# Another issue order for an attention and two-MoE kernel: 100 planning passes, three disturbed replays, mended instruction costs

## The chip, the cores and the metric

The kernel runs on one core of a Trainium2 chip. A core has a matmul engine (TensorE, PE in the profile; its weight loads are listed as PEld), VectorE (DVE), ScalarE (ACT), GpSimd (POOL) and SyncE (SP), which here issues the DMA transfers. Each engine works through its own queue in a fixed order; engines wait for each other through semaphores. The metric is the device time of one execution in microseconds (us).

## The reference

```python
# q, k, v: (4, 8, 576, 64) float32
q_d = q.reshape(B, H, Sd, 4, D).mean(axis=3)      # k_d, v_d alike: sequence pooled by 4
out_d = softmax(q_d @ k_d.T / sqrt(D)) @ v_d
out_up = np.repeat(out_d, 4, axis=2)
mask = np.abs(pos[:, None] - pos[None, :]) < 4    # a band of +-3
out_local = softmax(where(mask, q @ k.T / sqrt(D), -1e9)) @ v
x = (out_up + out_local) as (2304 tokens, 512)
# MoE1: w_in (512, 2048), w_out (2048, 512), alpha (2048)
h = x @ w_in
x = (np.maximum(h, 0) + alpha * np.minimum(h, 0)) @ w_out
# MoE2: w_gate, w_val (512, 1536), w_out (1536, 512), rms_g (512)
xn = x / sqrt(mean(x * x) + 1e-6) * rms_g
g = xn @ w_gate
out = (g * sigmoid(g) * (xn @ w_val)) @ w_out
```

The weights arrive as 64-bit floats and are decoded on the chip.

## The kernel before

**Numbers.** The large products take fp32 operands as two fp16 parts, high and low, and do three fp16 matmuls (high x high, high x low, low x high). Making the two parts is called a split: ACT writes the high part (line 373), DVE the low one (line 374).

**Weights.** A piece of a weight matrix (768 KB of 64-bit floats for the larger ones) is loaded as pairs of 32-bit words by SP (line 1091, tile `wr`), its high words are scaled by ACT (line 1110), its low words by ACT (line 1113), DVE joins the two (line 1115, tile `wc`) and the piece is then split into the tiles `wi`, `wo`, `w` or `w2` that the matmuls read. Lines 1110 and 1113 together are called the decode pair of a piece.

**Stages.** In the first 100 us, attention of batch 0 runs mostly on TensorE: q and k are loaded (line 743, tile `wo`), transposed by TensorE into PSUM tiles `tps` (line 792), written to SBUF by ACT (line 793, tile `T`), scored (lines 815, 868 to 880), exponentiated by ACT (lines 825, 900, tiles `dd` and `dls`) and multiplied with v. The local attention of batches 1 to 3 is done by DVE and POOL (products L478 and L526, sums L489 and L539), spread between later work. MoE1 takes blocks of 192 or 384 tokens: `hps` = x @ w_in on TensorE (line 1371), `g` on ACT (1375), alpha on DVE (1377), a split, and a second product (1388). MoE2 takes blocks of 384 tokens: `gps` on TensorE (1488), `th` = tanh on ACT (1497), DVE (1499, 1502), a split (1508, 1509, tile `uhl`) and the product with w_out (1517); the output leaves at 1586.

**What sets the order.** The program is first written in a natural order. Then `issue_order` (from line 24, called at 1715) orders every engine's queue anew. It works out which instruction needs which, gives each a cost (`cost`), and plays the whole program through repeatedly: a pass back from the end gives priorities, a pass forward gives a schedule whose times feed the next pass. In the forward pass it also models the matmul engine's slow periods and the port that DVE and POOL share. The order of the pass that ends first is kept, and each engine's queue is chained in it (`add_manual_dep`), the DMA queue of SP too. So the numbers in `cost` and the choice of pass set the order, and nothing else of the program.

Of the kernel before, what the change touches and what calls it, by code (L numbers as in the profile page):

```python
# [20 lines left out]
    return bass.AP(tensor=ap.tensor, offset=ap.offset + off, ap=[p] + [list(d) for d in dims])  # L21


def issue_order(tc, nc, groups, rounds=40):


    insts = [i for i in nc.cur_bb.bb.instructions if i.opcode != "TilePoolBoundary"]
    count = range(len(insts))
# [6 lines left out]
    def free(a):  # L35
        n = 1
        for _, c in list(a.ap)[1:]:
            n *= c
        return n
# [7 lines left out]
    def wide(a):  # L47
        return 2 if "16" in str(a.dtype) else 4

    def psum(a):  # L50
        return "PSUM" in str(a.tensor.space)

    def span(a):
        if psum(a):
            return 0, 128, 0, 1 << 20
        p, lo = divmod(a.offset, row(a))
        hi = lo + 1 + sum(abs(s) * (n - 1) for s, n in list(a.ap)[1:])
        return p, p + a.ap[0][1], lo * wide(a), hi * wide(a)
# [19 lines left out]
    def transfer(o, i):  # L78
        sides = [[c for _, c in a.ap if c > 1] or [1] for a in (o, i)]
        rings = max(x for x in range(1, 17) if not any(s[0] % x for s in sides))  # L80
        n = max(runs(a)[0] for a in (o, i))
        each = 4.0 * min(runs(a)[1] for a in (o, i))
        share = n / 16 * (10.0 + 0.046 * each)
        return max(share, n / rings * (9.0 + 0.042 * each)), max(share, 600.0)

    def cost(k, ins, outs):
        i, e = insts[k], eng[k]
        if not outs:
            return 60.0
        o, n = outs[0], free(outs[0])  # L90
        if e == "SP":
            return transfer(o, ins[0])[0]
        if e == "PE":
            if wide(ins[0]) == 2:
                return n / 2.4 + (2.5 if n > 128 else 50)
            return n * 2 / 2.4 + 4 if i.is_transpose else n * 4 / 2.4 + 100
        n = max([n] + [free(a) for a in ins[:1]])
        extra = len([a for a in ins[1:] if free(a) == 1 and n > 1])
        if e == "Activation":
            return (51 if psum(ins[0]) else 93) + n / 1.2 + 93 * (extra + len(outs) - 1)  # L100
        if e == "DVE":
            if i.opcode == "Reciprocal":
                return 89 + 6.25 * n
            fast = i.opcode in ("TensorScalarPtr", "TensorCopy") and not any(psum(a) for a in ins)
            fast = fast and len([a for a in ins if free(a) > 1]) < 2
            return 89 + n / (1.92 if fast else 0.96) + 60 * (extra > 0)
        if i.opcode == "TensorTensor":
            return 148 + n * (1.667 if any(list(a.ap)[-1][0] == 0 for a in ins) else 2.104)
        return 36 + 0.83 * n if i.opcode == "Memset" else 370 + 6 * n if i.opcode == "ISA" else 200 + 2.0 * n

    aps = [tuple([a.bass_ap for a in l if hasattr(a, "bass_ap")] for l in (i.ins, i.outs)) for i in insts]
    dur = [cost(k, *aps[k]) for k in count]

    held = [transfer(aps[k][1][0], aps[k][0][0])[1] if eng[k] == "SP" and aps[k][1] else None for k in count]

    def second(k, ins):
        if eng[k] == "Pool":
            return bool(ins)
        if eng[k] != "DVE" or not ins:
            return False  # L120
        n = len([a for a in ins if free(a) > 1 and not psum(a)])
        if n > 1:
            return True
        return insts[k].opcode in ("TensorScalarPtr", "TensorCopy") and not any(psum(a) for a in aps[k][0] + aps[k][1])

    shared = [second(k, aps[k][0]) for k in count]
# [6 lines left out]
    for names in ring.values():  # L133
        names = sorted((n for n in names if n in users), key=lambda n: users[n][0])
        kept = []
        for x, n in enumerate(names):
            old = {users[names[x - 1]][0]} if x else set()
            if len(kept) == slots[n]:
                done = [h for h in kept if users[h][-1] < users[n][0]]
# [5 lines left out]
    preds = [set() for _ in count]  # L145
    writes, reads, bank, first = {}, {}, {}, {}
    for k, (ins, outs) in enumerate(aps):
        for l, wr in ((ins, False), (outs, True)):
            for a in l:
                n = a.tensor.name  # L150
                if n not in slots:
                    continue
                s = span(a)
# [18 lines left out]
    succs = [[] for _ in count]  # L172
    at = {i.name: k for k, i in enumerate(insts)}
    mate, joined, fixed = {}, set(), [0.0] * len(insts)
# [22 lines left out]
    def lag(a, b):  # L197
        return 2300 if eng[a] == "SP" else waits.get((eng[a], eng[b]), 100)

    engines = sorted(set(eng))  # L200
    WIN, BUSY = 3413.0, 2900
    work = [0 if eng[k] != "PE" or not aps[k][1] else
            free(aps[k][1][0]) * (1 if wide(aps[k][0][0]) == 2 or insts[k].is_transpose else 2) for k in count]

    def run(P, S, prio, fwd, d):
# [33 lines left out]
                        heapq.heappush(soon[eng[s]], (at[s], s))  # L239
        return end, seq, real  # L240

    prio, d, best = [float(-k) for k in count], dur, None
    for _ in range(rounds):
        end = run(succs, preds, prio, False, d)[0]
        end, seq, d = run(preds, succs, [-x for x in end], True, dur)
        prio = [-x for x in end]
        if best is None or max(end) < best[0]:
            best = max(end), seq
    info = mybir.DependencyInfo(mybir.DependencyClass.NoSync, mybir.DependencyReason.DATA)
    for q in best[1].values():  # L250
        for a, b in zip(q, q[1:]):
# [4 lines left out]
def kernel(  # L256
# [1453 lines left out]
    for kind, m in (("m2", 0), ("m2", 1), ("m1", 2), ("m1", 3), ("m2", 2), ("m2", 3), ("m1", 4), ("m1", 5), ("m2", 4), ("m2", 5)):  # L1710
        if kind == "m1":
            m1(m, 0, BW, sl((kind, m)))
        else:
            m2(m, sl((kind, m)))
    issue_order(tc, nc, groups)


# [28 lines left out]
```

## Time and profile before

| | |
|---|---|
| median of 3 runs | 969.99 us (968.99 to 970.92) |
| the profiled execution | 967.56 us, of which its span 965.8 us |
| mean granted matmul clock | 0.991 of full speed |
| PE busy | 929.6 us (96% of the span) |
| DVE busy | 685.5 us (71%) |
| ACT busy | 481.7 us (50%) |
| POOL busy | 117.5 us (12%) |
| moved by DMA | 73.80 MB, 76 GB/s on average |

Busy shares are averages over the whole span, and the stages differ: which engine is full in which stretch is to be read from the stretches themselves. The median of the runs is 2.4 us above the profiled execution.

### The profile page before, as it was taken

What the parts mean: (1) busy time and instruction counts of PE and PEld (TensorE: products, weight loads), DVE (VectorE), ACT (ScalarE), POOL (GpSimd) and SP (SyncE); (2) the same over time, 40 slices, a digit from 0 to 9 for tenths busy, and PEclk for the clock granted to TensorE, in tenths of its full rate; (3) what the DMA queues carried; (4) which work ended last, traced back from release to release, by engine and by line L of the source; (5) the groups of instructions that cost most, each with busy time, mean ns of one, the idle gap of its engine ahead of it and who ended that gap; (6) DMA issues with size and microseconds to landing.
All of it is one profiled execution on the core that took longest, in us unless ns stands there. A gap on an engine that the chain in (4) does not pass through costs nothing.

```text
span 965.8 us, 16581 instructions
## 1 busy us (share of the span) xinstructions
PE 929.6 (96%) x6484; PEld 600.2 (62%) x6484; DVE 685.5 (71%) x1447; ACT 481.7 (50%) x1108; POOL 117.5 (12%) x96
## 2 busy tenths in 40 slices
PE   6978999999999999999999999999999999999998
PEld 4767777799655555565566655555556666555554
DVE  4789996998999978999987899963333442542333
ACT  5999889889864273233575322221322433321322
POOL 1101100201021103333102313210000000000000
PEclk9978999999999999999999999999999999999999
DMA  8886534574302142122122211000000000000000
GB/s 207 253 274 181 161 100 137 197 226 155 128 1 58 52 141 95 44 72 62 45 85 73 82 38 36 22 22 1 20 14 1 1 1 1 1 1 10 24 1 33
DMA packets 53712, 73.80 MB, mean 76 GB/s; under 512 B 22190, under 2 KB 35138, under 8 KB 53634
## 3 DMA queue, kind: packets, MB, share of 16 engines
q1 hardware_dynamic: 53634, 72.74, 24.9%
q8 instruction: 51, 0.84, 0.4%
q14 instruction: 27, 0.22, 0.1%
HBM read 68.01 MB, written 4.72 MB: 75 GB/s over the span
## 4 chain that ended last, share of the span: by engine, by line
PE 67%; DVE 13%; ACT 9%; issue 6%; DMA 5%; POOL 0%; SPq 0%; ACTq 0%; POOLq 0%
PE gps L1488 23%; PE hps L1371 12%; PE acc L1388 12%; PE oacc L1517 11%; DMA out_dram<-ob 4%; DVE prod L539 2%; DVE ls L489 1%; ACT wr L1110 1%; ACT dls L900 1%; DVE prod L526 1%; ACT wr L1113 1%; ACT wi L373 1%; DVE ghl L374 1%; DVE prod L478 1%; DVE hps L1377 1%
## 5 line engine op out<-in xcount | busy, mean ns | idle before, releaser
L1371 PE MATMUL hps<-xt,wi 128*128 128x192 f16 (+1 forms) x1536 | 357.0, 290 | 7.2 <-DVE g L374 3.8
L1488 PE MATMUL gps<-x,w 128*128 128x384 f16 x1728 | 339.0, 326 | 3.3 <-DVE th L1499 3.0
L1388 PE MATMUL acc<-ghl,wo 128*128 128x384 f16 (+1 forms) x960 | 253.8, 310 | 1.7 <-DVE ghl L374 0.6
L1488 PEld LDWEIGHTS <-w 128*128 128x128 f16 x1728 | 169.9, 99 | 118.4 <-issue 5.2
L1517 PE MATMUL oacc<-w,uhl 128*128 128x512 f16 x630 | 191.5, 379 | 2.3 <-ACT ob L1573 1.6
L1371 PEld LDWEIGHTS <-wi 128*128 128x128 f16 x1536 | 149.5, 100 | 59.4 <-issue 7.3
L1388 PEld LDWEIGHTS <-wo 128*128 128x128 f16 x1344 | 129.0, 98 | 61.7 <-issue 4.5
L1377 DVE SCALAR_TENSOR_TENSOR hps<-g,oma,hps 128x192 f32<-128x192 f32 (+1 forms) x128 | 66.0, 516 | 61.3 <-ACT g L1375 61.0
L1497 ACT ACTIVATE th<-gps,tsc 128x384 f32<-128x384 f32 x72 | 41.8, 580 | 132.3 <-PE gps L1488 131.8
L1517 PEld LDWEIGHTS <-uhl 128*128 128x128 f16 x630 | 61.6, 98 | 67.3 <-issue 2.4
L1499 DVE SCALAR_TENSOR_TENSOR th<-th,gps 128x384 f32<-128x384 f32 x72 | 39.6, 550 | 87.8 <-ACT th L1497 87.4
L1375 ACT ACTIVATE g<-hps 128x384 f32<-128x384 f32 x96 | 47.3, 493 | 84.1 <-PE hps L1371 83.5
L1508 ACT ACTIVATE uhl<-gps 128x384 f16<-128x384 f32 x72 | 41.7, 579 | 94.3 <-DVE gps L1502 85.5
L478 POOL TENSOR_TENSOR prod<-cq,ckv 128x896 f32<-128x896 f32 x24 | 54.8, 2284 | 191.6 <-DVE ls L489 50.6
L1388 PE MATMUL acc<-g,wo 128*128 128x384 f16 (+1 forms) x384 | 70.4, 286 | 0.0
L373 ACT ACTIVATE ghl<-hps,grp 128x384 f16<-128x384 f32 (+1 forms) x73 | 42.0, 576 | 51.2 <-DVE hps L1377 48.6
L1509 DVE TENSOR_TENSOR uhl<-gps,uhl 128x384 f16<-128x384 f32 x72 | 45.3, 629 | 28.1 <-ACT uhl L1508 27.8
L526 POOL TENSOR_TENSOR prod<-ls,ckv 128x896 f32<-128x896 f32 x24 | 43.6, 1816 | 163.3 <-DVE lo L539 70.6
L539 DVE TENSOR_TENSOR prod<-prod 128x384 f32<-128x384 f32 (+1 forms) x96 | 59.4, 630 | 4.3 <-POOL prod L526 4.3
L374 DVE SCALAR_TENSOR_TENSOR ghl<-hps,grp,ghl 128x384 f16<-128x384 f32 (+1 forms) x73 | 44.3, 607 | 23.9 <-ACT ghl L373 23.6
L489 DVE TENSOR_REDUCE ls<-prod 128x14 f32<-128x896 f32 x48 | 51.1, 1075 | 0.1
L1110 ACT ACTIVATE wr<-wr 128x768 f32<-128x768 f32 (+1 forms) x48 | 41.8, 877 | 6.2 <-DMA wr<-in_moe_w_out_dram 3.2
(242 smaller groups left out, 1138.9 us busy)
## 6 DMA issues: line engine op xcount, KB each, us to landing
wr<-in_moe_w_out_dram SPq DMA_DIRECT2D x18, 512.0 KB
wr<-in_moe_w_in_dram SPq DMA_DIRECT2D x10, 768.0 KB
wr<-in_moe_w_gate_dram SPq DMA_DIRECT2D x8, 768.0 KB
wr<-in_moe_w_val_dram SPq DMA_DIRECT2D x8, 768.0 KB
ckv<-in_k_dram SPq DMA_DIRECT2D x7, 768.0 KB
ckv<-in_v_dram SPq DMA_DIRECT2D x7, 768.0 KB
wr<-in_moe_w_out_dram SPq DMA_DIRECT2D x20, 256.0 KB
sd<-in_q_dram SPq DMA_DIRECT2D x24, 144.0 KB
```

What stands on the lines that cost most here:

```text
L373: nc.scalar.activation(out=hi, in_=src, func=AF.Copy, scale=s)
L374: nc.vector.scalar_tensor_tensor(out=lo, in0=src, scalar=s, in1=hi, op0=ALU.mult, op1=ALU.subtract)
L478: engs[i].tensor_tensor(out=pr, in0=view(st["q"][:, j, t:t + TP], [[D, TP], [0, ND], [1, D]]), in1=view(st["k"][:, j, t:t + TP], [[D, TP], ...
L489: nc.vector.tensor_reduce(out=st["s"][:, j, t:t + TP], in_=st.pop(("p", i)), axis=AX.X, op=ALU.add)
L526: engs[i].tensor_tensor(out=pr, in0=view(st["s"][:, j, t:t + TP], [[ND, TP], [1, ND], [0, D]]), in1=view(st["v"][:, j, t:t + TP], [[D, TP] ...
L539: add = lambda o, a, c: nc.vector.tensor_tensor(out=o, in0=a, in1=c, op=ALU.add)
L1110: nc.scalar.activation(out=hi.bitcast(F32), in_=hi.bitcast(F32), func=AF.Prelu, scale=2.0 ** -112, alpha=2.0 ** 32)
L1371: nc.tensor.matmul(ps[:, j], wi[:, f + j, a, kk * 128:(kk + 1) * 128], x[:, b_, kk, c0:c0 + n], start=(i == 0), stop=(i == 3 * KK - 1))
L1377: nc.vector.scalar_tensor_tensor(out=ps[:, j], in0=g[:, j], scalar=oma[:, f + j:f + j + 1], in1=ps[:, j], op0=ALU.mult, op1=ALU.add)
L1388: nc.tensor.matmul(acc[e], wo_f(f)[:, a, e * 128:(e + 1) * 128], hl[:, b_], start=(f == f0 and i == 0), stop=(f == f1 and i == 2))
L1488: nc.tensor.matmul(ps, w2_t[i0 + f // 3].rearrange("p a (k c) -> p a k c", k=KK)[:, a, kk, (f % 3) * 128:(f % 3 + 1) * 128], xh[:, b_, kk] ...
L1517: nc.tensor.matmul(acc[tt], t[:, a, tt * 128:(tt + 1) * 128], w[:, b_, f % 3], start=(f in first and i == 0), stop=(f in last and i == 2))
```

## The change

Only `issue_order` is changed; lines behind it stand 35 further down in the new file (L793 becomes L828, L374 becomes L409). Three things are new: 100 passes in place of 40; costs of some kinds of instruction (small fp16 and fp32 matmuls, transposes, ACT reading with a stride or writing 16 bits, DVE reading PSUM with a stride, and a floor for short DVE instructions); and the choice among the passes, which takes those that end less than 8 us after the best mean so far, plays their orders through three times with disturbed costs of ACT, DVE and SP, and keeps the order with the least mean end. No instruction is added or removed on any engine.

```diff
-def issue_order(tc, nc, groups, rounds=40):
+def issue_order(tc, nc, groups, rounds=100):
...
-                return n / 2.4 + (2.5 if n > 128 else 50)
-            return n * 2 / 2.4 + 4 if i.is_transpose else n * 4 / 2.4 + 100
+                return max(25.0, n / 2.4 + 2.5)
+            return n * 2 / 2.4 + 3 if i.is_transpose else n * 4 / 2.4 + (128 if n < 64 else 8)
...
-            return (51 if psum(ins[0]) else 93) + n / 1.2 + 93 * (extra + len(outs) - 1)
+            odd = ins and not psum(ins[0]) and list(ins[0].ap)[-1][0] != 1
+            return ((51 if psum(ins[0]) else 93) + n / (1.09 if odd else 1.2) + 93 * (extra + len(outs) - 1)
+                    + 20 * (wide(o) == 2))
...
-            return 89 + n / (1.92 if fast else 0.96) + 60 * (extra > 0)
+            if ins and psum(ins[0]) and list(ins[0].ap)[-1][0] > 2:
+                return 69 + n / 0.58
+            return max(150, 69 + n / (1.92 if fast else 0.96) + 60 * (extra > 0))
...
+    def replay(seq, factors, phase):
+        by = dict(zip(("Activation", "DVE", "SP"), factors))
...
+            f = by.get(e, 1.0)
+            x = f * dur[k]
...
+    trials = (((1.0, 1.0, 1.0), 0.0), ((1.03, 1.0, 1.1), 1700.0), ((1.0, 1.03, 0.95), 800.0))
...
-        if best is None or max(end) < best[0]:
-            best = max(end), seq
+        if best is None or max(end) < best[0] + 8000.0:
+            x = sum(replay(seq, *a) for a in trials) / len(trials)
+            if best is None or x < best[0]:
+                best = x, seq
```

What it moves is told by the order of instructions. POOL's queue stays as it was. TensorE's is the same from the MoE1 blocks 4 and 5 on, about 700 us from the start, and nearly the same from the second MoE2 block on, about 345 us. Three places follow.

**SP, the first DMA transfers.** Loads of q and k, and the first pieces of w_in (`wr`). Before:

```order
L743 DMA wo<-in_q_dram 96x6x64
L743 DMA wo<-in_k_dram 96x6x64
L743 DMA wo<-in_q_dram 96x6x64 x2
L743 DMA wo<-in_k_dram 96x6x64
L1650 DMA rows<-in_moe_alpha_dram 16x128
L1650 DMA rows<-in_moe_rms_g_dram 4x128
L743 DMA wo<-in_k_dram 96x6x64
L743 DMA wo<-in_q_dram 96x6x64
L1091 DMA wr<-in_moe_w_in_dram 128x2x768
```

Of the change:

```order
L778 DMA wo<-in_q_dram 96x6x64
L778 DMA wo<-in_k_dram 96x6x64
L778 DMA wo<-in_q_dram 96x6x64
L1126 DMA wr<-in_moe_w_in_dram 128x2x768
L778 DMA wo<-in_k_dram 96x6x64
L778 DMA wo<-in_q_dram 96x6x64
L778 DMA wo<-in_k_dram 96x6x64
L1126 DMA wr<-in_moe_w_in_dram 128x2x768
```

The first piece of w_in was the 14th transfer of SP's queue and is the 6th; the second was the 19th and is the 10th.

**ACT, its start.** `T0` are the transposed q and k of the first heads, `dd` the first exponentials, `wr_661` and `wr_663` the first two pieces of w_in. Before, from the second write of `T0` on:

```order
L793 ACTIVATE T0_183<-tps_275 128x3x96
L793 ACTIVATE T0_183<-tps_281 128x3x96
L793 ACTIVATE T0_183<-tps_286 128x3x96
L793 ACTIVATE T0_188<-tps_292 128x3x96
L793 ACTIVATE T0_188<-tps_297 128x3x96
L793 ACTIVATE T0_188<-tps_303 128x3x96
L825 ACTIVATE dd_314,dsum_324<-sps_317,dm_323 72x144
L825 ACTIVATE dd_314,dsum_324<-sps_318,dm_323 72x144
L793 ACTIVATE T0_188<-tps_308 128x3x96
L825 ACTIVATE dd_314,dsum_324<-sps_317,dm_323 72x144
L825 ACTIVATE dd_314,dsum_324<-sps_318,dm_323 72x144
L1110 ACTIVATE wr_661<-wr_661 128x768
```

Of the change, from the same place:

```order
L828 ACTIVATE T0_183<-tps_275 128x3x96
L1145 ACTIVATE wr_661<-wr_661 128x768
L1148 ACTIVATE wr_661<-wr_661,nhalf_99 128x768
L828 ACTIVATE T0_183<-tps_281 128x3x96
L828 ACTIVATE T0_183<-tps_286 128x3x96
L828 ACTIVATE T0_188<-tps_292 128x3x96
L1145 ACTIVATE wr_663<-wr_663 128x768
L1148 ACTIVATE wr_663<-wr_663,nhalf_99 128x768
L828 ACTIVATE T0_188<-tps_297 128x3x96
```

Two decode pairs now stand between the writes of the first two heads; before, the first stood behind all of them.

**ACT, at a group of MoE1 near 95 us.** `g_1214` reads the product `hps_1189`; TensorE needs the split that follows (`g0_1119`) and the freed PSUM. Before:

```order
L1375 ACTIVATE g_1214<-hps_1189 128x384
L900 ACTIVATE dls_1437,dlsum_1434<-lsps_1419,dlm_1433 96x102
L900 ACTIVATE dls_1437,dlsum_1434<-lsps_1420,dlm_1433 96x102
L900 ACTIVATE dls_1437,dlsum_1434<-lsps_1419,dlm_1433 96x102
L900 ACTIVATE dls_1437,dlsum_1434<-lsps_1420,dlm_1433 96x102
L900 ACTIVATE dls_1437,dlsum_1434<-lsps_1419,dlm_1433 96x102
L900 ACTIVATE dls_1437,dlsum_1434<-lsps_1420,dlm_1433 96x102
L373 ACTIVATE xt_498<-dls_972,sc_104 128x192
L373 ACTIVATE g0_1119<-hps_1189,sc_104 128x2x192
```

Of the change:

```order
L1410 ACTIVATE g_1214<-hps_1189 128x384
L1148 ACTIVATE wr_1294<-wr_1294,nhalf_99 128x256
L961 ACTIVATE laT_1228<-ltps_1223 102x384
L408 ACTIVATE wi_106<-wc_790,swi_112 128x512
L961 ACTIVATE laT_1235<-ltps_1230 102x384
L408 ACTIVATE xt_498<-dls_889,sc_104 128x192 x2
L408 ACTIVATE g0_1119<-hps_1189,sc_104 128x2x192
```

`g_1214` now stands ahead of eight ACT instructions that were ahead of it (six of them in these rows), and the six exponentials stand behind the split.

**DVE, in the first MoE2 block near 260 us.** `th_3768` waits for TensorE's `gps_3755` and frees what TensorE needs next; `w2` is a weight split, `prod` and `lo` are local attention. Before:

```order
L1302 TENSOR_TENSOR ra_3674<-ra_3674,ra_3797 128x384
L1499 SCALAR_TENSOR_TENSOR th_3768<-th_3768,gps_3755 128x384
L1509 TENSOR_TENSOR uhl_3725<-gps_3711,uhl_3725 128x384
L1502 SCALAR_TENSOR_TENSOR gps_3771<-th_3768,gps_3771 128x384
L374 SCALAR_TENSOR_TENSOR w2_3693<-wc_3676,sw2_118,w2_3693 128x1536
```

Of the change:

```order
L574 TENSOR_TENSOR prod_4107<-prod_4107 128x2x2x64
L401 TENSOR_SCALAR eb2_117<-s2_114 128x1
L1337 TENSOR_TENSOR ra_3674<-ra_3674,ra_3728 128x384
L1291 SCALAR_TENSOR_TENSOR inv2_122<-eb2_117 128x1
L1544 TENSOR_TENSOR uhl_3725<-gps_3711,uhl_3725 128x384
L409 SCALAR_TENSOR_TENSOR w2_3809<-wc_3745,sw2_118,w2_3809 128x1536
L1337 TENSOR_TENSOR ra_3674<-ra_3674,ra_3797 128x384
L1534 SCALAR_TENSOR_TENSOR th_3768<-th_3768,gps_3755 128x384
```

Ahead of `th_3768` now stand, beside what stood there, two weight splits of 128x1536 (`w2_3809`, here, and `w2_3693`, further up), the `uhl` split, four pieces of local attention (one `prod` of 128x384, two of 128x256, one `lo`) and seven instructions on a column of 128x1. The same holds, with other instructions, for the `th` steps around it in this block; by the second MoE2 block both orders have the same work ahead.

## Rows read from the trace of the kernel before

**Rows 1.** Busy time per engine, clock and DMA by stretch (columns in the first row).

```profile
core 0: us, PE busy (x) PEld busy (x) DVE busy (x) ACT busy (x) POOL busy (x), PEclk, DMA share, GB/s
10.00:60.00 50.00, 44.50 (x339) 35.16 (x337) 34.20 (x100) 43.29 (x131) 4.88 (x4) 0.93 0.87 257
60.00:110.00 50.00, 40.34 (x439) 34.63 (x440) 46.91 (x113) 47.49 (x131) 8.27 (x12) 0.90 0.63 183
110.00:255.00 145.00, 143.91 (x1488) 120.83 (x1485) 128.22 (x299) 131.35 (x280) 14.79 (x10) 1.00 0.51 161
255.00:345.00 90.00, 86.22 (x517) 49.70 (x515) 88.13 (x187) 44.06 (x85) 12.95 (x6) 1.00 0.21 65
700.00:966.00 266.00, 259.55 (x1534) 150.29 (x1531) 100.11 (x183) 79.55 (x145) 0.00 (x0) 1.00 0.03 8
```

**Rows 2.** What PE waited for, whole run: us in total, times, longest us.

```profile
PE hps L1371 <- DVE g L374: 3.8, 5, 1.6
...
PE gps L1488 <- DVE th L1499: 3.0, 4, 1.0
```

**Rows 3.** ACT's timeline, 8 to 20 us: start, duration, instruction, idle before.

```profile
8.20 1.18 ACT L793 ACTIVATE T<-tps 128x288 f32<-128x288 f32 x2 [6.11 <-PE tps L792]
10.05 1.18 ACT L793 ACTIVATE T<-tps 128x288 f32<-128x288 f32 x2 [0.67 <-PE tps L792]
11.90 0.68 ACT L793 ACTIVATE T<-tps 128x288 f32<-128x288 f32 x1 [0.67 <-PE tps L792]
14.30 0.67 ACT L793 ACTIVATE T<-tps 128x288 f32<-128x288 f32 x1 [1.72 <-PE tps L792]
15.57 0.67 ACT L793 ACTIVATE T<-tps 128x288 f32<-128x288 f32 x1 [0.60 <-PE tps L792]
...
17.86 0.90 ACT L1110 ACTIVATE wr<-wr 128x768 f32<-128x768 f32 x1
18.65 0.67 ACT L793 ACTIVATE T<-tps 128x288 f32<-128x288 f32 x1
19.11 0.96 ACT L1113 ACTIVATE wr<-wr,nhalf 128x768 int32<-128x768 uint32 x1
19.95 0.35 ACT L900 ACTIVATE dls<-lsps,dlm 96x102 f32<-96x102 f32 x1
```

**Rows 4.** SP's timeline: issue of the first piece of w_in.

```profile
9.38 0.63 SPq L1091 DMA_DIRECT2D wr<-in_moe_w_in_dram  x1
```

**Rows 5.** Stretches from the start, columns as in rows 1; last number is GB/s.

```profile
0.00:6.20 6.20, 0.93 (x4) 0.72 (x4) 1.06 (x9) 1.28 (x1) 2.05 (x26) 1.00 0.54 123
0.00:10.50 10.50, 3.54 (x16) 2.56 (x16) 1.81 (x10) 2.91 (x4) 2.05 (x26) 1.00 0.67 146
0.00:15.10 15.10, 7.86 (x42) 5.64 (x42) 3.68 (x16) 4.99 (x7) 2.05 (x26) 1.00 0.74 183
12.00:14.00 2.00, 2.00 (x18) 1.63 (x18) 0.07 (x2) 0.58 (x1) 0.00 (x0) 1.00 0.96 345
```

**Rows 6.** PE's timeline near 95 to 102 us.

```profile
96.61 0.90 PE L1371 MATMUL hps<-xt,wi 128*128 128x192 f16 x9 [0.61 <-DVE g L374]
...
101.69 0.57 PE L1371 MATMUL hps<-xt,wi 128*128 128x192 f16 x5 [1.56 <-DVE g L374]
```

**Rows 7.** The stretch 50 to 80 us, columns as in rows 1.

```profile
50.00:80.00 30.00, 23.24 (x203) 19.81 (x202) 24.76 (x57) 29.74 (x78) 0.00 (x0) 0.72 0.77 251
```

**Rows 8.** The stretch 200 to 260 us, columns as in rows 1.

```profile
200.00:260.00 60.00, 59.19 (x624) 52.66 (x622) 55.24 (x121) 53.44 (x79) 5.12 (x3) 1.00 0.50 164
```

**Rows 9.** DVE's timeline near 260 us, and POOL's instruction beside it.

```profile
261.48 0.54 DVE L1499 SCALAR_TENSOR_TENSOR th<-th,gps 128x384 f32<-128x384 f32 x1
...
262.87 1.80 DVE L374 SCALAR_TENSOR_TENSOR w<-wc,sw,w 128x1536 f16<-128x1536 f32 x1
...
266.40 0.27 DVE L539 TENSOR_TENSOR lo<-prod 128x128 f32<-128x128 f32 x1
...
267.12 1.97 DVE L539 TENSOR_TENSOR lo<-prod 128x128 f32<-128x128 f32 x1
...
266.80 2.15 POOL L478 TENSOR_TENSOR prod<-cq,ckv 128x896 f32<-128x896 f32 x1 [13.79 <-DVE lo L539]
```

More of the change, by code (lines that the diff above doesn't have):

```diff
@@ L240, in run @@
         return end, seq, real
+    def replay(seq, factors, phase):
+        by = dict(zip(("Activation", "DVE", "SP"), factors))
+        pos, clock = dict.fromkeys(engines, 0), {e: 2100.0 if e == "Activation" else 600.0 for e in engines}
+        left, at = [len(p) for p in preds], [0.0] * len(insts)
+        port, last = 0.0, 0.0
+        win, done, slow = 0, 0, True
+        for _ in count:
+            t, e = min((max(clock[e], at[seq[e][pos[e]]]), e) for e in engines
+                       if pos[e] < len(seq[e]) and not left[seq[e][pos[e]]])
+            k = seq[e][pos[e]]
+            pos[e] += 1
+            f = by.get(e, 1.0)
+            x = f * dur[k]
+            if e == "PE":
+                while t + phase >= (win + 1) * WIN:
+                    slow, win, done = done < BUSY, win + 1, 0
+                done += work[k]
+                x = (2 * x - 2.5 if slow else x) + fixed[k]
+            if shared[k]:
+                x += max(0.0, port - t)
+                port = t + x
+            last = max(last, t + x)
+            clock[e] = t + (x if held[k] is None else f * held[k])
+            for s in succs[k]:
+                left[s] -= 1
+                at[s] = max(at[s], t + x + lag(k, s))
+        return last
+    trials = (((1.0, 1.0, 1.0), 0.0), ((1.03, 1.0, 1.1), 1700.0), ((1.0, 1.03, 0.95), 800.0))
     prio, d, best = [float(-k) for k in count], dur, None
```

## The prediction

> **What bounds the kernel now.** No instruction is added or removed, so only waiting can change. I read first the table of stretches, since idle time of TensorE (PE) is all that another order can win. From 110 to 255 us PE is busy 143.91 of 145 us: nothing to win there. It idles 5.5 us in 10 to 60 and 9.7 us in 60 to 110 (50 less the busy time), 3.8 us in 255 to 345 and 6.5 us in 700 to 966 [rows 1]. The last of these is out of reach, because PE's order is the same there before and after.
>
> Second, who is full where PE idles. In 60 to 110 ACT is busy 47.49 of 50 us and DVE 46.91; in 10 to 60 ACT is busy 43.29 [rows 1], and in 50 to 80 it is busy 29.74 of 30 while PE has 23.24 [rows 7]. So there ACT sets the pace: its decodes, splits and exponentials feed the matmuls. In 255 to 345 DVE is busy 88.13 of 90 [rows 1]. Third, PE's waits: the largest that recurs is hps (MoE1's first product) for the split behind g, 3.8 us in 5 waits, then gps (MoE2's first product) for th, 3.0 us in 4 [rows 2]. Last, the timelines at the places where the order changes: at the start ACT, the later bottleneck, still idles 0.67 + 0.67 + 1.72 + 0.60 = 3.66 us between writes of transposed q and k [rows 3].
>
> **The start: ACT's idle time is filled.** The change puts two decode pairs into exactly these gaps. One pair costs what it pushes back on ACT: the next row starts 0.79 us after the first instruction of the pair (18.65 less 17.86) and 0.84 us after the second (19.95 less 19.11), so 1.63 us; two pairs 3.3 us [rows 3]. This fits in the 3.66 us. Everything on ACT after 16 us can then stand 3.3 us earlier, and where ACT is full, that is what PE gains.
>
> What it costs. The first pair stands behind the first two writes, which end at 8.20 + 1.18 = 9.38. It ends at 11.0, and the next writes, at 10.05 before, start 1.0 us late [rows 3]; the gaps behind can take that up again. But the piece must also have landed by 9.38, which is the time at which it was only issued before [rows 4]. Bytes: ahead of it stand five loads of q and k (96x384 floats, 147 KB each), 0.74 MB; the piece is 0.79 MB, together 1.52 MB. Early bound: 0.74 MB had come by 6.2 us (123 GB/s from the start), and the piece at 345 GB/s, the rate of 12 to 14 us, takes 2.3 us more: 8.5. Late bound: 1.52 MB had come at 10.5 us (146 GB/s from the start) [rows 5]. If late, the pair ends at 12.1 and the writes are 2.1 us behind. I take 1.0 us lost, halfway between 0 and 2.1 (landing at 9.5, about when ACT asks). Since the transfers are only exchanged, the sum of bytes by 20 us is the same; alpha and the rms weights come later, and nothing here reads them before the first g. The loads of q and k that stand behind the two pieces come later by up to 2.3 us a piece; the transposes that need them are the price of the first rival.
>
> Term one: -3.3 + 1.0 = -2.3 us, bounds -3.3 (nothing lost) and -0.9 (the second piece late as well, rival A below).
>
> **MoE1 near 95 us: g earlier.** Eight ACT instructions no longer stand ahead of g_1214, and six exponentials no longer stand between it and its split. PE waits there for the split twice, 0.61 and 1.56 us [rows 6]. What is late next is DVE, which makes the low half of the split and is itself busy 46.91 of 50 us [rows 1]; so not the whole wait goes. Bounds 0 and -2.2; I take half, -1.1 us. The exponentials that moved back feed a local attention product that PE reads later, with other matmuls at hand; I cost that at nothing, and if that cover is gone it takes back what this term gives.
>
> **50 to 80 us: the clock.** PE's granted clock has a mean of 0.72 there [rows 7]: a mix of the two levels, with 2 x 0.28 x 30 = 16.8 us at the lower one (1.2 GHz), after stretches in which PE idled. If all of it went or as much came again, the busy time would change by about half of 16.8 x 23.24/30 = 13.0, so 6.5 us either way. As ACT is full there, a faster PE would only wait longer: I take 0. The Trainium skill, TensorE: Matmul & The Clock Gate, section "What's actually happening", says that the default state is throttled and that activity releases the throttle; by that a denser PE would win back some of these 6.5 us, and the trace agrees in that the clock is 1.00 in every row where PE is busy without gaps. That outcome is a part of the third rival.
>
> **110 to 345 us: DVE's order in the first MoE2 block.** Ahead of th_3768 stand more: two weight splits of 128x1536 at 1.80 us, one uhl and one prod of 128x384 at 0.54 (the nearest row is th, of that size), two prods of 128x256 at 0.41 (between 0.27 for 128x128 and 0.54), one lo at 0.27 [rows 9]: 3.60 + 1.08 + 0.82 + 0.27 = 5.8 us, the columns of 128x1 left out. PE has the same work ahead of its gps_3755. It is the same DVE work, only earlier, so it is covered if DVE gets there that much ahead. It idles 60 - 55.24 = 4.8 us in 200 to 260 [rows 8], which is where it could be taken in; and an ACT that runs 2.3 us ahead gives DVE its inputs sooner. I take 0: the nearest row, the idle time, covers 4.8 of the 5.8, and the lead of term one the rest. Bounds: +5.8 without cover; -3.0 if all waits of gps for th go [rows 2]. From 345 us on PE's order is nearly the same and from 700 us identical: 0.
>
> **Sum.** -2.3 - 1.1 + 0 + 0 = -3.4 us, so 967.56 - 3.4 = 964.2 for a profiled execution. The median of the runs is 969.99, 2.4 us above it; I carry the difference over: 966.6.
>
> **Rivals.**
>
> A, the lead is eaten at the start. The second piece has eight loads ahead and the first piece: 1.18 + 2 x 0.79 = 2.75 MB. Early bound 8.5 + 1.23 MB / 345 GB/s = 12.1 us; late bound 15.1 us, when 2.75 MB had come (183 GB/s from the start) [rows 5]. ACT wants it behind the write that starts at 11.90, so about 12.9 with the delay above. At the late bound its pair ends at 15.1 + 1.63 = 16.7 and the write that stood at 14.30 [rows 3] is 2.4 us late, with the first delay in it. Then 3.3 - 2.4 = 0.9 us is left, and with nothing won near 95 us (DVE full) the time is 969.1. For it: ACT must now wait in order for a transfer, where before it only idled. Against it: 345 GB/s were reached, twice the average of the first 15 us, and large pieces come more densely than short loads. Chance 0.23.
>
> B, slower: DVE stops PE in the first MoE2 block. The 5.8 us ahead of th_3768 and its neighbours are not covered; DVE is busy 88.13 of 90 us in 255 to 345 [rows 1], and gps waits for th already, 3.0 us [rows 2]. It decides from the point where DVE reaches th after PE has filled the PSUM tiles of gps, that is once the 4.8 us of idle time are used up. Then +5.8 on -3.4: 972.4. Against it: PE can go on with products of MoE1 that wait for nothing, and DVE has the lead of the stage before. One thing may make it worse: a lo of 128x128 took 0.27 us alone and 1.97 us while POOL ran its product [rows 9], so moved pieces of local attention may fall beside POOL. The Trainium skill, GPSIMD Engine Reference, section "Specifications", states that POOL shares its SBUF interfaces with DVE, with contention against DVE instructions of two SBUF inputs; lo is such an instruction, and the row agrees. Chance 0.18.
>
> C, a larger gain: everything in 10 to 110 us closes up. PE idles 100 - 44.50 - 40.34 = 15.2 us there [rows 1]; after the -3.4 some 11.8 remain. If another third goes, 3.9 us, or as much of the 6.5 us at the lower clock, the time is 962.7. For it: ACT full means that each of its moves tells on PE. Against it: the pieces of ACT's work are the same, and DVE is nearly as full. Chance 0.17.
>
> **How the numbers follow.** The forecast has 0.42, with its own range 964.5 to 968.8: nothing lost at the start and all of the 2.2 us near 95 won (-5.5), or 2.1 lost and nothing won there (-1.2). What can be told from no change is about 0.2%, 1.9 us: 968.05 to 971.93. Faster: 0.37 of the forecast, 0.04 of A, 0.17 of C, so 0.58. The same: 0.05 of the forecast, 0.16 of A, 0.04 of B, so 0.25. Slower: 0.03 of A and 0.14 of B, so 0.17. The range reaches down to C with the rest of the wait near 95 us (962.7 - 1.1, so 961.5) and up to B (972.5); the bounds of the clock lie beyond it.
>
> **What the profile of the changed kernel would show.** Term one: the two decode pairs on ACT between 9 and 15 us, ACT's gaps there gone, no wait for the transfer of wr over 1 us, and by 50 us ACT's instructions some 2 us earlier; wrong, if ACT waits for wr_663 until 15 us. Term two: hps waits for the split under 2.7 us in all. The zero in 255 to 345: gps waits for th no longer than 3.0 us, and PE's idle time there is at most 3.8 us. The prediction fails as a whole if PE's idle time in 10 to 110 us stays at 15 us, or if the loss turns up behind 345 us, where I count nothing.

## The result: 0.7% slower

The changed kernel took 976.0 us in the median of 8 runs (971.78 to 978.68), the kernel before 968.76 (967.87 to 970.92) beside it: ratio 1.0069, 95% interval 1.0047 to 1.0091. The forecast was 966.6; the time lies above the range. The profiled execution took 978.07 us, span 976.4, so it is 2 us above the median, as the one of before was below its own.

The stretches of [rows 1], in the trace of the change (columns: PE, PEld, DVE, ACT and POOL busy, granted clock, DMA share, GB/s):

```profile
10.00:60.00 50.00, 45.47 (x325) 35.27 (x325) 32.62 (x91) 41.48 (x129) 5.00 (x4) 1.00 0.83 241
60.00:110.00 50.00, 39.33 (x438) 33.66 (x439) 47.20 (x120) 46.30 (x118) 6.94 (x10) 0.93 0.60 185
110.00:255.00 145.00, 138.48 (x1410) 117.06 (x1410) 121.81 (x286) 126.16 (x283) 14.85 (x11) 0.96 0.52 163
255.00:345.00 90.00, 87.40 (x546) 52.69 (x544) 86.75 (x188) 47.34 (x83) 13.96 (x7) 1.00 0.15 48
700.00:966.00 266.00, 264.08 (x1569) 154.25 (x1568) 102.45 (x189) 81.88 (x150) 0.00 (x0) 1.00 0.03 7
```

In this trace the loss shows where nothing was to be won: 110 to 255 us has 6.5 us of idle PE (145 less 138.48) against 1.1, and a clock of 0.96 against 1.00. In 10 to 110 us PE's idle time is 15.2 us, as it was before: that is the first of the two signs by which the prediction said that it would fail as a whole. (In 700 to 966 PE is busier only because the later program leaves its tail outside.)

Cut finer, the change (first fence) and before (second), in the five stretches that count:

```profile
0.00:20.00 20.00, 10.40 (x62) 7.65 (x63) 7.75 (x25) 10.87 (x21) 2.04 (x26) 1.00 0.91 215
...
110.00:165.00 55.00, 51.72 (x495) 40.37 (x495) 44.81 (x123) 48.19 (x138) 1.69 (x2) 0.94 0.44 131
...
240.00:260.00 20.00, 15.43 (x147) 13.64 (x145) 18.42 (x36) 18.06 (x24) 4.02 (x2) 0.91 0.40 119
260.00:345.00 85.00, 84.28 (x521) 50.49 (x519) 81.75 (x179) 43.13 (x78) 11.63 (x6) 1.00 0.16 51
...
430.00:460.00 30.00, 26.61 (x164) 15.98 (x163) 30.00 (x46) 7.54 (x14) 10.39 (x5) 1.00 0.09 28
```

```profile
0.00:20.00 20.00, 12.47 (x69) 8.88 (x69) 7.37 (x30) 9.42 (x21) 2.69 (x27) 1.00 0.82 196
...
110.00:165.00 55.00, 55.00 (x557) 43.22 (x555) 47.42 (x128) 50.43 (x135) 0.00 (x0) 1.00 0.50 148
...
240.00:260.00 20.00, 19.44 (x153) 13.48 (x151) 18.83 (x33) 17.02 (x27) 2.07 (x2) 1.00 0.41 137
260.00:345.00 85.00, 81.22 (x490) 47.08 (x488) 83.13 (x177) 41.64 (x81) 12.95 (x6) 1.00 0.18 56
...
430.00:460.00 30.00, 28.64 (x178) 17.40 (x176) 29.99 (x54) 9.72 (x19) 9.99 (x5) 1.00 0.19 57
```

PE's busy time is 2.1 us less in the first 20 us, 3.3 less in 110 to 165 (with the clock at half for part of it), 4.0 less in 240 to 260 (the clock again), 2.0 less in 430 to 460, and 3.1 more in 260 to 345, where part of the loss comes back.

The start itself did what the order says. ACT's timeline of the change, to be laid beside [rows 3]:

```profile
8.32 1.18 ACT L828 ACTIVATE T<-tps 128x288 f32<-128x288 f32 x2 [6.23 <-PE tps L827]
9.63 0.90 ACT L1145 ACTIVATE wr<-wr 128x768 f32<-128x768 f32 x1
10.43 1.00 ACT L1148 ACTIVATE wr<-wr,nhalf 128x768 int32<-128x768 uint32 x1
11.50 1.22 ACT L828 ACTIVATE T<-tps 128x288 f32<-128x288 f32 x2
13.39 0.68 ACT L828 ACTIVATE T<-tps 128x288 f32<-128x288 f32 x1 [0.67 <-PE tps L827]
13.92 0.90 ACT L1145 ACTIVATE wr<-wr 128x768 f32<-128x768 f32 x1
14.72 0.97 ACT L1148 ACTIVATE wr<-wr,nhalf 128x768 int32<-128x768 uint32 x1
```

Both pieces had landed in time: up to 15.7 us ACT idles 0.67 us, where it idled 3.66 by 16.2, and it waits for no transfer. The lead did not last. In 0 to 50 us ACT has done less than before, not more (the change, then before):

```profile
0.00:50.00 50.00, 39.64 (x267) 30.66 (x268) 27.28 (x86) 34.30 (x97) 7.04 (x30) 1.00 0.82 222
```

```profile
0.00:50.00 50.00, 39.16 (x270) 30.48 (x272) 29.32 (x89) 36.01 (x102) 6.93 (x30) 1.00 0.85 232
```

ACT is busy 34.30 us with 97 instructions, against 36.01 with 102; up to 60 us it waits 3.8 us for `dlm`, a step of the local attention on DVE, against 1.0 before. The price of the early pieces is on PE, in what it waited for (whole run of the change; us in total, times, longest):

```profile
PE tps L827 <- DMA wo<-in_q_dram: 3.8, 1, 3.8
PE hps L1406 <- DVE g L409: 3.8, 3, 2.8
...
PE vqps L631 <- DMA sd<-in_v_dram: 2.1, 2, 1.5
PE tps L827 <- DMA wo<-in_k_dram: 2.0, 1, 2.0
```

The wait for q is the one for the first load, 3.6 us before. The wait for k, 2.0 us, is new: that load stood ahead of the w_in piece and now stands behind it. The wait of hps for the split behind g is 3.8 us in all as in [rows 2], but it has moved: 2.8 of it fall in 60 to 90 us. That of gps for th, 3.0 us before, is gone; other waits have its place, ahead of the first MoE2 block. In 240 to 260 us, where PE waited 0.3 us at most for any one thing before:

```profile
PE gps L1523 <- DVE ghl L409: 1.9, 1, 1.9
PE acc L1423 <- ACT ghl L408: 1.3, 1, 1.3
PE hps L1406 <- DVE ghl L409: 1.2, 2, 0.6
```

`ghl` is the split of the last MoE1 groups.

### The profile page after: what moved, and what is told of

The parts are those of the page before. It is cut to its first block, busy times and chain, and to the rows that moved or that the text cites. A ratio compares the mean times of both kernels' runs of the same rounds, so it can differ in the third digit from the quotient of the medians.

```text
span 976.4 us, 16576 instructions
## 1 busy us (share of the span) xinstructions
PE 932.4 (96%) x6484; PEld 603.0 (62%) x6484; DVE 686.4 (70%) x1447; ACT 482.0 (49%) x1108; POOL 114.2 (12%) x96
## 4 chain that ended last, share of the span: by engine, by line
PE 74%; DVE 9%; DMA 7%; ACT 6%; issue 1%; SPq 1%; ACTq 0%; DVEq 0%
PE gps L1523 26%; PE acc L1423 13%; PE oacc L1552 13%; PE hps L1406 12%; DMA out_dram<-ob 4%; DVE prod L574 2%; DMA wr<-in_moe_w_val_dram 1%; PE lsps L915 1%; DVE ghl L409 1%; DVE hps L1412 1%; ACT wr L1145 1%; PE tps L827 1%; PE sps L692 1%; DVE ls L524 1%; DMA sd<-in_v_dram 1%
## 5 line engine op out<-in xcount | busy, mean ns | idle before, releaser
L1406 PE MATMUL hps<-xt,wi 128*128 128x192 f16 (+1 forms) x1536 | 341.6, 290 | 9.4 <-DVE ghl L409 4.0
L1523 PE MATMUL gps<-x,w 128*128 128x384 f16 x1728 | 345.1, 326 | 2.1 <-DVE ghl L409 1.9
L1423 PE MATMUL acc<-ghl,wo 128*128 128x384 f16 (+1 forms) x960 | 244.6, 311 | 2.5 <-ACT ghl L408 2.2
L1552 PE MATMUL oacc<-w,uhl 128*128 128x512 f16 x630 | 196.2, 379 | 1.7 <-ACT ob L1608 1.7
L513 POOL TENSOR_TENSOR prod<-cq,ckv 128x896 f32<-128x896 f32 x24 | 51.9, 2163 | 200.8 <-DVE ls L524 55.2
L1423 PE MATMUL acc<-g,wo 128*128 128x384 f16 (+1 forms) x384 | 72.8, 290 | 0.0
L409 DVE SCALAR_TENSOR_TENSOR ghl<-hps,grp,ghl 128x384 f16<-128x384 f32 (+1 forms) x73 | 44.3, 607 | 21.8 <-ACT ghl L408 21.5
```

Source lines behind the costliest of these rows:

```text
L409: nc.vector.scalar_tensor_tensor(out=lo, in0=src, scalar=s, in1=hi, op0=ALU.mult, op1=ALU.subtract)
L513: engs[i].tensor_tensor(out=pr, in0=view(st["q"][:, j, t:t + TP], [[D, TP], [0, ND], [1, D]]), in1=view(st["k"][:, j, t:t + TP], [[D, TP], ...
L1406: nc.tensor.matmul(ps[:, j], wi[:, f + j, a, kk * 128:(kk + 1) * 128], x[:, b_, kk, c0:c0 + n], start=(i == 0), stop=(i == 3 * KK - 1))
L1423: nc.tensor.matmul(acc[e], wo_f(f)[:, a, e * 128:(e + 1) * 128], hl[:, b_], start=(f == f0 and i == 0), stop=(f == f1 and i == 2))
L1523: nc.tensor.matmul(ps, w2_t[i0 + f // 3].rearrange("p a (k c) -> p a k c", k=KK)[:, a, kk, (f % 3) * 128:(f % 3 + 1) * 128], xh[:, b_, kk] ...
L1552: nc.tensor.matmul(acc[tt], t[:, a, tt * 128:(tt + 1) * 128], w[:, b_, f % 3], start=(f in first and i == 0), stop=(f in last and i == 2))
```

## The experiments

Each run's order was given as a table, so that one part of either order could be kept. The kernel before ran beside each; ratios are to it. "Up to X" means: what stands ahead of PE's first matmul of X in one order, then the rest in the other.

**Splices near 105 and 210 us.** Theory P: the loss sits at places of the order and the start gains 3.3 us. Rival L: PE, being ahead, runs into loads of v that land when they did, and stalls there whatever the order.

```diff
-before throughout
+e1: change up to hps_1377 (105 us), then before
+e2: before up to hps_1377, then change
+e3: change up to hps_3196 (210 us), then before
+e4: before up to hps_3196, then change
```

> Every queue in the order of the change up to the first matmul of hps_1377 (about 100 us), from there on in the order of before. Theory P (the loss sits at places of the order): by the traces the change has lost less PE time than before by 110 us (idle time and half of the time at the lower clock: 26.2 us against 29.5), and that 3.3 us should stay: about 965.5 us. Rival L (the lead itself is the trouble: PE, 3 us earlier, runs into v loads that land when they did, idles at 110 to 120 us and drops to the lower clock, whatever the order there): 970 to 973 us, with a low-clock stretch near 120 us.

Measured 977.29 us, ratio 1.0076 (1.0062 to 1.0089). Theory P fell as it stands: the order of the start alone, with this cut behind it, loses as much as all of the change.

> Every queue in the order of before up to hps_1377, from there on in the order of the change. Theory P: the change without its gain at the start, so all of its losses: 976 + 3.3, about 979 us, with PE idle and at half clock near 120 us and idle again at 240 to 260 and 440 to 460. Rival L: no lead, so no wall at 110 to 130 us: what is left are the losses at 240 to 260 and 440 to 460, about 973 us.

974.50 us, 1.0054 (1.0033 to 1.0075): neither 979 nor clearly 973.

> Every queue in the order of the change up to the first matmul of hps_3196 (about 200 us), from there on in the order of before. Theory P: gain of the start 3.3, loss at 110 to 130 of 2.8 idle and up to 3.4 from the lower clock: 968.8 - 3.3 + 2.8 to 6.2, so 968.3 to 971.7. Rival L: the same, since the lead and the wall are both in: this run does not tell the two apart, it sizes the loss before 200 us beside the first run.

983.47 us, 1.0128 (1.0103 to 1.0153), slower than either theory allows. The profiled execution took 976.81, 6.7 us less than the median, so its trace shows only a part; just at the seam it has:

```profile
210.00:225.00 15.00, 9.88 (x89) 9.14 (x87) 9.89 (x25) 8.42 (x14) 0.00 (x0) 0.77 0.59 209
```

PE, DVE and ACT all idle there: the two orders have different work behind them at that cut, and the cut itself costs. So none of e1 to e4 sizes anything by itself: the cut near 105 us is of this kind too, and e4 is cut at the same place as e3 (PE idles 2.7 us there in 210 to 225).

> Every queue in the order of before up to hps_3196, from there on in the order of the change. Theory P: only the later losses: 240 to 260 us (4.5 idle and 1.7 from the lower clock against 0.5 before, 2.6 of it given back at 290 to 340) and 440 to 460 (3.1 idle against 0.3), so +3 to +6: 972 to 975 us. Rival L: the later places are stalls of a DVE that was made late by the first one; with that gone they shrink: 968 to 970 us.

975.38 us, 1.0051 (1.0033 to 1.0069), the top of theory P. PE idled 5.7 us in 240 to 260 and 3.1 in 440 to 460: the later stalls come without any lead ahead of them, so L fell as well, by the trace more than by the time.

**One part of the change by itself.**

```diff
 e5: SP and ACT of the kernel before, at the start
-L743 k, alpha, rms, k, q, L1091 wr_661 ... L1091 wr_663 (14th and 19th transfer)
+wr_661 6th, wr_663 10th; decode pairs behind the 2nd and the 5th write of T
 e6: DVE of the change, near 250 us
-prod, lo of local attention (7 rows) ... ghl_3539
+ghl_3539 ... prod, lo (7 rows)
 e7
-def issue_order(tc, nc, groups, rounds=40):
+def issue_order(tc, nc, groups, rounds=100):
 e8: cost() of the change, rounds=40, least max(end)
```

> The kernel before with one part of the change: SP's first 25 transfers in the order of the change, and the decode pairs of the first two w_in pieces where the change has them on ACT; all other rows in the order of before. By the prediction's term one: -2.3 us (bounds -3.3 to -0.9), so 966.5 to 968.9. Rival G (the pairs fit, but the lead ends in a later wait, since in the first run the start of the change alone won nothing): 969 to 971 us, with PE's idle time in 60 to 120 us as large as before, or larger.

973.80 us, 1.0028 (1.0012 to 1.0043): term one has the wrong sign. Its trace, first 20 us and 60 to 110, then PE's waits in the first 20 us:

```profile
0.00:20.00 20.00, 7.60 (x41) 5.48 (x41) 4.43 (x17) 8.38 (x11) 2.04 (x26) 1.00 0.90 197
...
60.00:110.00 50.00, 40.11 (x432) 33.89 (x431) 46.92 (x114) 50.00 (x139) 6.22 (x10) 0.88 0.65 194
```

```profile
PE tps L792 <- DMA wo<-in_q_dram: 4.4, 1, 4.4
PE tps L792 <- DMA wo<-in_k_dram: 3.2, 1, 3.2
```

PE lost 4.9 us at the start (7.60 busy against 12.47). In 60 to 110 it is busy 40.11 us against 40.34 [rows 1]: the early decodes gave nothing back there. Here ACT did wait for the pieces, unlike in the trace of the change:

```profile
ACT wr L1110 <- DMA wr<-in_moe_w_in_dram: 2.2, 2, 1.1
```

> The change with seven DVE instructions of local attention (prod and lo, 3.2 us) moved behind the split ghl_3539, so that the last splits of MoE1 before the first MoE2 block come earlier on DVE. Theory D (these rows hold PE at 240 to 257 us, 4.5 us idle there): idle time there falls by 2 to 3 us; as the same DVE work returns behind, where the change has idled less than before (0 against 3.7 at 260 to 340), 1 to 3 us of it stay: 973 to 975 us. Rival E (the wait only passes to the next rows, ACT's decodes among them, which stand ahead too): 976 us or more, idle time at 240 to 270 us unchanged.

978.87 us, 1.0085 (1.0057 to 1.0113). Rival E: PE is busy 15.40 us in 240 to 260, as without the edit, and behind it gps waits for another row (in an execution of 985.14 us, the slowest of the six):

```profile
PE gps L1488 <- ACT x L1402: 4.3, 1, 4.3
```

> The order that 100 passes give with the old costs (the choice by three replays picks the same pass there as the least end). Theory N (before is a good draw among orders that the planner rates nearly alike, and another draw loses 3 to 9 us whatever made it): 972 to 978 us. Rival M (the mended costs make the loss): 968 to 970 us here, and 974 or more in the run with the costs alone.

972.67 us, 1.0021 (1.0006 to 1.0036).

> The order that 40 passes and the old choice (least end) give with the new costs. Theory N: 972 to 978 us, as in the run with passes alone. Rival M (the costs make the loss): 974 to 978 here and 968 to 970 with passes alone. Rival Q (the further passes make it, by fitting the planner's model more closely): 968 to 970 here and 974 or more with passes alone.

977.86 us, 1.0072 (1.0054 to 1.0091). The costs alone lose what the change loses, the passes alone a third of it. That does not make the costs the cause: both times lie in the range of theory N, by which before is a good draw among orders that the planner rates nearly alike, while rival M wanted 968 to 970 for e7. The third part did nothing: with the costs of either kernel, 100 passes give the same order whether the three replays choose or the least end does.

**Splices where the orders agree.** Near 70, 165 and 395 us the two orders have almost the same instructions behind them (5, 16 and 1 differ), so I took the cuts for clean.

```diff
+e9:  change up to tps1_2429 (165 us), then before
+e10: before, change from tps1_2429 to gps_5267 (395 us), before
+e11: before up to gps_5267, then change
+e12: change up to sqps_776 (70 us), then before
+e13: change, before from tps1_2429 to gps_5267, change
```

> The order of the change up to the transposes tps1_2429 (about 165 us; the two orders have there almost the same work behind them, 1.8 us of it differing, so the seam is clean, unlike at 105 and 210 us), from there on that of before. Theory D2 (three places lose, and add up): here the start's loss (PE waits 2 to 5 us longer for k in the first 20 us, as seen in the run with the early pairs alone) less what 20 to 60 us give back (2 us): +0 to +4, so 970 to 974 us, the upper end where the lower clock falls at 110 to 130 us. By the prediction: -3.4, 967. Rival W (nothing but the dirty seams lost in the first two runs): 969 to 970 us.

974.32 us, 1.0042 (1.0020 to 1.0065).

> The order of the change only from the transposes tps1_2429 (165 us) to the MoE2 group gps_5267 (395 us, where the two orders differ by 0.2 us of work), that of before outside. Theory D2: idle time at 240 to 257 us, 4 us more than before, 2.5 us given back at 260 to 340, and a low-clock stretch in some runs: +1.5 to +4, so 971.5 to 974.5 us. By the prediction's zero for this stage: 970. By its rival B (all 5.8 us): 976.

976.47 us, 1.0079 (1.0055 to 1.0102): more than I expected by then. A part of it is the clock's. Three of the six runs had a mean clock of 0.989 to 0.991, as the kernel before has, and took 973.2 to 974.9 us, 3.9 to 5.6 over before; the three with 0.979 to 0.986 took 978.1 to 981.3. The trace (979.75 us, clock 0.979), 240 to 260 and 260 to 345 us:

```profile
240.00:260.00 20.00, 15.41 (x147) 13.86 (x145) 18.41 (x36) 18.61 (x24) 4.03 (x2) 0.87 0.43 136
260.00:345.00 85.00, 85.00 (x525) 51.23 (x523) 80.01 (x175) 42.50 (x71) 11.65 (x6) 0.99 0.16 49
```

> The order of before up to the MoE2 group gps_5267 (395 us), from there on that of the change. Theory D2: the idle time at 437 to 457 us, 3.1 us against 0.3 to 1.4: +2 us, so 972 to 973. By the prediction's zero from 345 us on: 970.

971.16 us, 1.0020 (1.0010 to 1.0031): the part to which I gave zero loses 2 us, at the expected place (PE busy 26.80 us in 430 to 460, DVE 30.00 of 30).

> The order of the change up to the weight sums sqps_776 (about 70 us, a clean seam, 2.3 us of work differing), from there on that of before. Theory D2: the start's loss and what 20 to 60 us give back: +0 to +2, so 970 to 972 us. If the early pairs alone are what loses in the run up to 165 us, both runs read alike; if the loss comes at 105 to 130 us, this one is near 970 and the other 3 us above.

973.83 us, 1.0039 (1.0018 to 1.0060), about as much as e9: as far as the intervals tell, the first 70 us hold the whole loss up to 165.

> The order of the change, but from the transposes tps1_2429 (165 us) to the MoE2 group gps_5267 (395 us) that of before. Apart, the three stretches of the change cost 4.1, 7.7 and 1.9 us over before, 13.7 together, yet the whole change costs 7.2 in its first job. If stretches add in the whole, taking out the middle one leaves 4.1 + 1.9: 975 us; and if the middle one costs its 7.7 there too, 976 - 7.7: 968. Theory O (a stretch whose stall is a DVE and ACT that come late costs less behind a PE that is late already, so the middle one is worth only 1 to 2 us in the whole): 974 to 976 us. Theory V (it costs 4 us or more in the whole too, and the two others less): 968 to 972.

974.69 us, 1.0050 (1.0030 to 1.0070), in the range of theory O, though its interval and that of the whole change overlap. It is also about what e9 and e11 lose together (4.1 + 1.9), so it does not show theory O's reason, that a stall costs less behind a PE that is late already. It says that the middle stretch is worth little in the whole change: about 2 us by the two ratios, within the noise.

**The start, taken apart.**

```diff
 e14: SP of the kernel before, first 25 transfers in the change's order; ACT as before
 e15: ACT of the kernel before; SP as before
-T0<-tps_297, T0<-tps_303, dd ..., wr_661 pair
+wr_661 pair, T0<-tps_297, T0<-tps_303, dd ...
```

> The order of before with SP's first 25 transfers in the order of the change; ACT as before. If the transfers alone make the loss of the early pairs (q, k and rms loads that land behind two w_in pieces of 0.79 MB: PE idle 12.4 us in the first 20 against 7.5), then +2 to +4 here too: 971.5 to 973.5 us, PE's wait for k in the first 20 us 2 to 5 us. If the ACT pairs between the writes of T make it, no loss: 969 to 970 us, idle time in the first 20 us under 8.5.

972.41 us, 1.0024 (1.0011 to 1.0038): the transfers alone make nearly all of e5's loss. The first 20 us of e14, and two of PE's waits in them that before does not have:

```profile
0.00:20.00 20.00, 9.55 (x51) 6.80 (x51) 4.93 (x22) 6.64 (x14) 2.05 (x26) 1.00 0.91 208
```

```profile
PE tps L792 <- DMA wo<-in_k_dram: 1.6, 1, 1.6
PE vecps L1653 <- DMA rows<-in_moe_rms_g_dram: 1.1, 1, 1.1
```

> The order of before, with only the decode pair of the first w_in piece on ACT moved three writes of T earlier, into ACT's gap at 12.6 to 14.3 us; SP as before, so no load lands later. If an earlier ACT pays at all when no load is pushed back: -1 to -1.6 us, 968 to 969 us. If the piece, issued at 9.38, has not landed by 12.6 and ACT waits with the writes behind it: +1 to +3 us. If ACT's lead is worth nothing, as the end of the first 110 us is set by DVE and by transfers: 969 to 970.5 us.

971.14 us, 1.0013 (1.0002 to 1.0025): the piece had not landed, and ACT waited with the writes of T behind it:

```profile
ACT wr L1110 <- DMA wr<-in_moe_w_in_dram: 2.9, 1, 2.9
```

**The rows at 250 us.**

```diff
 DVE of the change (e16), of e10 (e17)
-w2_3464, hps_3474, prod_4042, hps_3474 ... s2, lo, sw2, wc_3873, hps_3540, ghl_3473
+hps_3474, hps_3474, w2_3464, prod_4042 ... ghl_3473, s2, lo, sw2, wc_3873, hps_3540
```

> The change, with three DVE rows of the last MoE1 groups moved: the two hps_3474 rows ahead of the weight split w2_3464 (1.8 us) and a prod, and the low half ghl_3473 ahead of the five rows that held it (1.5 us of work, while its high half was ready). Theory H (these rows hold PE at 240 to 260 us, where in the change it idles 4.5 us): idle time there 1 to 2.5 us, and since the whole stretch is worth only about 2 us in the whole change, 974 to 975 us. If other rows hold it: idle time 4 us or more, 976 or above.

977.81 us, 1.0082 (1.0059 to 1.0105); idle time in 240 to 260 grew to 7.9 us.

> The order of before with the change's only from 165 to 395 us, and the same three DVE rows moved. Without the move this stretch cost 7.7 us over before. Theory H: idle time at 240 to 260 us falls from 4.6 to 1 to 2.5 us and the time by 2 to 4 us: 972 to 974.5. If other rows hold PE there: 976 or above, and idle time 4 us or more.

978.45 us, 1.0091 (1.0059 to 1.0123). Theory H fell, though the low clock takes a part of e17's time too (0.980 to 0.987 in its four runs). In e17 the wait only changed its row, as PE's timeline shows:

```profile
258.20 0.32 PE L1488 MATMUL gps<-x,w 128*128 128x384 f16 x1 [0.16 <-DVE ghl L374]
...
264.56 0.38 PE L349 MATMUL allps<-s,ones 128*128 128x1 f32 x2 [2.77 <-ACT w L1124]
```

gps now waits 0.16 us for ghl, where in e10 it waited 1.88, but the sum of squares of a weight piece (L1124 on ACT, needed for the piece's scale) costs 2.77. ACT started it at 262.93, when a DVE split of 128x1536 had ended; by the order that is `w2_3598`, eight rows behind `ghl_3473`.

## Why the prediction was wrong

**Term one, -2.3 us, is the first step that failed.** It measured +2.7 us in e5 and +2.3 in e14, by the ratios. The pieces landed about when I said, in the change by 9.6 and 13.9 us, inside the bounds 8.5 to 10.5 and 12.1 to 15.1; in e5 ACT waited 2.2 us for them. Three things were wrong. I priced the landing of the pieces for ACT (1.0 us) and left "the loads of q and k that stand behind" to rival A, which then priced ACT's writes instead. PE waits for those loads directly: in the trace of every run with SP's early pieces it idles 9.4 to 12.4 us in the first 20, in every one with SP's and ACT's order of before 7.5 to 8.0 (e15, whose ACT waits, 9.8). I wrote that nothing reads alpha and the rms weights before the first g; PE reads them (`vecps`) at 14 to 15 us in the trace of before, and in e14 it waits 1.1 us for one of them. And I took ACT's lead for PE's: by 50 us ACT had no lead left in the change, and in e5 PE is busy no longer in 60 to 110 us than before, although ACT has 3.3 us of work behind it. A full engine at the end of a chain was no proof that its work, done earlier, lets anything else start earlier; DVE was busy 46.91 of 50 us there [rows 1], and I had held that against term two and rival C, not against term one.

**Term two, -1.1 us,** came at its place and was taken back there. PE's waits in 85 to 115 us, of the change and then of before:

```profile
PE ltps L959 <- POOL dls L945: 1.5, 2, 0.7
PE hps L1406 <- DVE g L409: 0.9, 2, 0.7
PE qkps L679 <- DVE qkp L669: 0.9, 1, 0.9
PE lops L971 <- ACT laT L961: 0.7, 1, 0.7
```

```profile
PE hps L1371 <- DVE g L374: 2.5, 3, 1.6
PE lops L936 <- ACT laT L926: 0.6, 2, 0.3
PE ltps L924 <- POOL dls L910: 0.5, 1, 0.5
```

The wait for the split behind g fell from 2.5 to 0.9 us, but those for attention grew from 1.1 to 3.1 (`dls` and `laT`, of the local one, from 1.1 to 2.2; `qkp` came new). I had costed the exponentials that moved back at nothing, on condition that other matmuls cover them; by these waits they did not. Which of the moved rows makes which of these waits was not tried.

**The zero for 110 to 345 us** missed as well, by an amount that stays open: 3.9 to 5.6 us alone in e10 at the clock of before, about 2 in the whole. Rival B came nearest, with DVE late for PE, but not with its row: the waits of gps for th are gone, and PE waits some 10 us earlier, for the splits of the last MoE1 groups. I let 4.8 us of DVE idle time in 200 to 260 cover the moved rows. That idle time is a sum over 60 us, and it did not keep PE from waiting at one point of them. In each trace with the change's order there PE idles 4.6 to 5.7 us in 240 to 260 (not counting the runs with edits at that place), in those with the order of before 0.6 to 1.9. Which rows make it is open: three edits moved the wait from ghl to x and to the squares of a weight piece, and none made the run faster.

**Zero from 345 us on** was wrong by 2 us (e11). That an order is nearly the same on PE says nothing of DVE, which is full there in both orders (30.00 and 29.99 us of 30).

**The clock.** I put its bounds at 50 to 80 us, where ACT hides it. In the change the lower level (1.2 GHz) came where PE sets the pace:

```profile
110.00:120.00 10.00, 7.13 (x85) 6.09 (x84) 7.17 (x27) 8.69 (x37) 1.69 (x2) 1.00 0.68 209
120.00:127.00 7.00, 6.97 (x41) 5.13 (x41) 5.58 (x14) 4.35 (x10) 0.00 (x0) 0.51 0.15 49
249.00:254.00 5.00, 4.67 (x37) 4.48 (x37) 5.00 (x10) 4.27 (x6) 0.00 (x0) 0.66 0.71 235
```

PE idles 2.9 us in 110 to 120 (part of it for the v loads), then works at 0.51 for 7 us: 3.4 us lost behind an idle time of 2.9. But e3, with the same order, has 1.00 in 110 to 165, and over the whole execution the mean clock is 0.991 before and after; how much of the 7 us is the clock's is not settled, since it falls in some executions and not in others. The spread of the change's runs does not follow the mean clock: the fastest (971.78 us) had 0.989, the slowest (978.68) 0.988.

**What is shown and what is not.** Shown: the start and the two later stretches each lose (e9 to e12), and SP's early pieces are more than half of the start's loss (e14: 2.3 us, of 3.8 in e12 and 4.1 in e9, by the ratios). Not shown: whether the parts add. Apart they are 4.1 + 7.7 + 1.9 by the ratios of e9 to e11, 6.7 together by that of the whole; but with e10's runs at the clock of before the sum is 10 to 12, and the intervals then hardly part the two. Not shown either: whether the new costs make the worse order or any other draw would (e7 and e8 both fit theory N).

## What to carry to other kernels

Price a transfer that is moved forward by who waits for the transfers it overtakes, not by whether it lands in time itself. An engine's lead is worth something only if the engine that ends last was waiting for it at that point, and idle time elsewhere in a stretch need not cover what is wanted now. Of the eighteen other orders timed here, fifteen of them mixtures or edits of two, none beat the one before, and the runs of one order differ by 0.2 to 1.2%: new costs in a planner are a reason to time its order, not to expect a gain.

## What the runs showed of the hardware that was not expected

In e10, and again in e17, the clock fell at 166 us and stayed at the lower level for 17 us although PE was busy throughout; e10 here:

```profile
150.00:166.00 16.00, 14.27 (x144) 11.10 (x142) 8.91 (x22) 14.71 (x43) 0.00 (x0) 1.00 0.56 161
166.00:183.00 17.00, 17.00 (x99) 11.41 (x98) 9.00 (x24) 9.02 (x31) 3.49 (x4) 0.51 0.26 80
183.00:200.00 17.00, 17.00 (x146) 12.27 (x144) 12.68 (x23) 12.47 (x19) 3.45 (x2) 0.99 0.61 199
```

PE had idled 1.7 us in the 16 us ahead, all of it in the last three. In the 17 us it did transposes and small products of local attention between those of MoE1 until 178 us, then MoE1 alone, and the clock rose at 183. By estimate half of PE's work of 17 us, 8 us, went there in this execution. The stretch begins right behind the cut of e10 and e17 at 165 us; in the traces of the change and of before the clock is 1.00 in 166 to 183 us, so it is no part of what the change lost in its own trace. The Trainium skill, TensorE: Matmul & The Clock Gate, section "What's actually happening", says that activity releases the throttle, the rule on which the third rival drew. Taken by busy time, this row does not bear it out: PE was busy 17.00 of 17 us, by a profile that models the ends of matmuls, at 0.51. What kept the clock down was not tried.
